# A fused attention and MLP block on one core: the first 220 jobs of a written-out job order in another sequence

## The chip, the core and the metric

The kernel runs on one core of one Trainium2 chip. The core has five engines with instruction queues of their own, each worked off in order: PE (matmul; its weight loads are listed as PEld), DVE (vector), ACT (activations), POOL (GpSimd) and SP, which here only issues DMAs. The metric is the device time of one execution in microseconds, the median of several runs. The profile is of one further execution, recorded instruction by instruction.

## What is computed

With x of 2048 rows by 512 columns, normalised to xn, the output is x + A(xn) + B(xn):

```python
# A: 32 heads of 16, 4 segments of 512 rows
q, k, v = heads(xn @ wq), heads(xn @ wk), heads(xn @ wv)
for s in range(4):
    p = softmax(q[s] @ k[s].T * scale + causal_mask)
    a_mem = (phi(q[s]) @ M) / (phi(q[s]) @ z + 1e-6)
    o[s] = g * a_mem + (1 - g) * (p @ v[s])
    M += phi(k[s]).T @ v[s];  z += phi(k[s]).sum(rows)
A = concat(o) @ wo
# B: a layer norm of its own, then two dense layers of width 1792
B = gelu(layernorm(xn) @ w1 + b1) @ w2 + b2
```

## The kernel before

**Split operands.** Products run as three float16 matmuls. Every weight and every row of xn is scaled and split into a high half and a low half in float16, and `split3` (L474 to L481) multiplies high by high, high by low and low by high into one PSUM bank. A group of 12 matmuls is thus a product over 512 inputs.

**What a weight needs first.** A weight matrix is loaded (`wl`, L245), its sum of squares is taken on ACT (`wm`, L311, each with a read-out of the accumulator), PE adds the sums over partitions by a matmul with ones and ACT takes a root (`wf`, L317 to L357: PE L326, L343 and L345, ACT L320 and L321, then short DVE operations), and then each piece of 128 rows or columns is split (`ws`, L359). There are two ways of splitting, by a letter in `SPLIT`: "V" is ACT L366 for the high half and DVE L367 for the low one; "G" is POOL L369 (scale), ACT L370 (high), POOL L371 (low). The weights come as the parts qk (first group of wq and wk), QK (the other three groups), v, 1a and 1b (the halves of w1), 2a and 2b (of w2), and o.

**The work.** Rows go in 4 segments of 512, heads in 4 groups of 8, so that there are 16 units (segment, group). For a unit, `T` projects k or q (`qk_proj`, L506: PE L480, ACT L514 and for a mapped k or q L517, DVE L518 to L530, and three stores to a scratch buffer in DRAM, from which four loads bring both back in another layout). `N` transposes phi(k), `V` projects v for 128 rows (PE L480 with wvs, ACT L593), `K` updates the state (PE L602). `M` finds row maxima of the scores (PE L621, DVE L628, 12 jobs a unit), `R` turns them (PE L499 with mc) and sends them through DRAM, `S` takes the exponentials (PE L661, ACT L666, POOL L675), `pv` and `PV` multiply by v (PE L690), and `O` normalises. For the MLP, `D` is one group of 12 matmuls of the first layer (PE L480 with w1s, DVE L756), `G` the gelu on ACT, `H` its split (POOL L770 and L772, ACT L771), and `e` a step of the second layer (PE L797). `X` and `Xt` normalise and transpose the rows, `ratio` lays out the row scales of the second norm, `gate` computes the gates from beta, and `warm` is eight matmuls of ones with no use of the result (L823).

**What sets the order.** No scheduler does. The kernel has 28 streams of jobs, each with a letter (`streams`, L57). `ORDER` is a string of 1307 letters: at each letter the next job of that stream is recorded on whichever engines it needs, and every engine keeps that order. `BANKS` is a string of digits that says, at each taking of a PSUM bank, which of the eight it is. The jobs are numbered from 0 here. Up to job 219 the kernel loads, checks and splits nearly all weights, projects units 0 and 1, finds their maxima and starts the exponentials and the MLP. Among the letters are a (norm), c (loads of weights), f and g (key and query projection), t (warm-up) and u to B (squares, scale and splits, one letter for each part of the weights).

```python
    for c in "".join(ORDER):
        key = next(todo[NAMES.index(c)])
```

Of the kernel before, what the change touches and what calls it, by code (L numbers as in the profile page):

```python
# [56 lines left out]
def streams():  # L57
# [42 lines left out]


ORDER = (
    "aatcucuccvavtctveecttcetcuvaactvuvtaatcattavdtubcwwvccfwxxcxwxyxyxxgyhxcoxxvwxofooowcvwzyzoiyyiazgyyziiynzoiiys"
    "ppAnziiniicvzvcniiooAzmAihiiopzqqiqcivpqjpqjijqqijizqjiqqjiiAwszBzoAskkkkmjiAojoijsoAijAqjqjasAfoAopgkkkkpjpjqq"
    "jlpoolojjjooilihAAkkkkpaiqqiqijqjqqijqjiqjqjisBfgpiiqkkkkmpliqqiooiqpBlqoBopohijjiojiijpolsjiqaqajqiqiqqiiqapka"
    "kmkktspaqijqiqjqiqajqbqajopijjgBfopkkkBkjjjlooooBlhjjjolqiqqiipkkkkjiqqijqqjjiqiqjjqiqiqiBkkkkmpliilfnplimpngrr"
    "mrjjponijqjqjinjipiskmkkmkaiijrijjoojiqsjqqjiqiiiqqkkkkihlqlfmlogojqjqjqqjjasoojmkkkkmqjiqjqjjaojjpipmooisikkkk"
# [9 lines left out]


BANKS = (
    "012345670123457063571265407321640573216405732164053271640527163054271630542713605427105472105427105472105472015"  # L120
    "470251407251405712470512470512470536124075631254076340125637123756123576132576132576132576132576135402761350427"
    "163054273106542736574326574326537425632754632574631072456310724563071245360712453620731620731067203617621073621"
    "073621073621037621037621037261702361475023671540263701524603175246031746013746013713460713471630471630463714067"
    "314056723410523674105236741052367410527410527410527410527410527140352671450326475103264751023674523674523647253"
# [786 lines left out]
```

## Time and profile before

| | us |
|---|---|
| median of 3 runs | 694.91 (694.29 to 697.16) |
| span of the profiled execution | 693.1 |
| PE busy | 678.7 (98%) |
| DVE busy | 535.4 (77%) |
| ACT busy | 522.7 (75%) |
| POOL busy | 347.2 (50%) |
| mean granted clock of PE | 0.995 |

The page states no time of the profiled execution beside its span; the span, from the first to the last instruction, is 1.8 us below the median of the runs. A row of the time line has the start, the time taken, the engine, the line of the kernel, the operation, output and inputs, the number of instructions merged in it, and in brackets the idle time of the engine ahead of it with what ended it. Times are from the start of the span.

### The profile page before, as it was taken

The numbers are of one execution on the slowest core, as the hardware profiler recorded it, in microseconds if no ns is written. First come the engines' busy times: TensorE is split into PE (matmuls) and PEld (weight loads), VectorE is DVE, ScalarE is ACT, GpSimd is POOL, SyncE is SP. The second block draws the span as 40 slices with busy tenths as digits, with TensorE's granted clock in tenths as the row PEclk, the third lists the DMA queues.
The fourth block names the chain that finished last, engine by engine and source line by source line (L and its number), as shares of the span: only waits on it lengthen the run. The fifth ranks groups of instructions, "written<-read, shape, count | busy, mean of one in ns | idle before, by whom it ended". The sixth has DMA issues, their size and how long they took to land.

```text
span 693.1 us, 16949 instructions
## 1 busy us (share of the span) xinstructions
PE 678.7 (98%) x6359; PEld 395.7 (57%) x6359; DVE 535.4 (77%) x1695; ACT 522.7 (75%) x1013; POOL 347.2 (50%) x533
## 2 busy tenths in 40 slices
PE   7799999999999999999999999999999999999997
PEld 6465556576654555566554456567564456656653
DVE  4499978897795887998798786888678595969442
ACT  5989898878795659857795697757795687778870
POOL 5276768365624425664334445454362546455752
PEclk9899999999999999999999999999999999999999
DMA  9984222420204213431113224231120416140101
GB/s 272 283 238 136 64 63 63 108 62 14 84 10 115 87 44 74 100 71 33 51 45 92 63 72 99 63 93 33 31 80 24 132 18 152 18 108 3 18 1 61
DMA packets 51790, 55.12 MB, mean 80 GB/s; under 512 B 4782, under 2 KB 40636, under 8 KB 51708
## 3 DMA queue, kind: packets, MB, share of 16 engines
q1 hardware_dynamic: 49404, 49.84, 25.3%
q0 software_dynamic: 2304, 4.20, 3.7%
q8 instruction: 50, 0.82, 0.5%
q14 instruction: 32, 0.26, 0.1%
HBM read 36.99 MB, written 17.04 MB: 78 GB/s over the span
## 4 chain that ended last, share of the span: by engine, by line
PE 78%; ACT 10%; POOL 4%; DVE 3%; issue 2%; DMA 1%; SPq 1%; POOLq 0%; ACTq 0%; DVEq 0%
PE ps L480 33%; PE ps L797 16%; PE ps L690 10%; PE ps L815 6%; PE ps L661 5%; PE ps L621 5%; ACT pt L666 2%; DVE ps L628 2%; PE ps L571 2%; PE ps L499 1%; ACT hT L763 1%; ACT hT L771 1%; SPq L252 1%; POOL w1s L371 1%; DMA pt<-in_A_wk_dram 1%
## 5 line engine op out<-in xcount | busy, mean ns | idle before, releaser
L628 DVE CUSTOM_DVE_ANT_0 ps<-ps,mask 128x512 f32<-128x512 f32 (+3 forms) x512 | 233.8, 522 | 16.1 <-PE ps L621 14.9
L666 ACT ACTIVATE pt<-ps,qkcs 128x512 f32<-128x512 f32 (+1 forms) x384 | 206.1, 624 | 35.3 <-PE ps L661 33.5
L797 PE MATMUL ps<-w2s,hT 64*128 64x512 f16 x1344 | 176.7, 376 | 0.2
L480 PE MATMUL ps<-xnT,w1s 128*128 128x256 f16 x1344 | 157.8, 273 | 0.0
L675 POOL TENSOR_SCALAR_AFFINE_SELECT pt<-pt 128x256 f32<-128x256 f32 x256 | 99.1, 414 | 92.0 <-ACT pt L666 91.0
L480 PEld LDWEIGHTS <-w1s 128*128 128x128 f16 x1344 | 127.3, 98 | 29.1 <-issue 11.3
L772 POOL TENSOR_TENSOR hT<-hh,hT 128x512 f16<-128x512 f32 x64 | 67.8, 1059 | 82.8 <-ACT hT L771 81.0
L797 PEld LDWEIGHTS <-hT 64*128 64x128 f16 x1344 | 76.3, 94 | 50.7 <-issue 6.0
L690 PE MATMUL ps<-pt,vt 128*32 128x512 f32 (+3 forms) x1024 | 77.3, 435 | 0.1
L756 DVE SCALAR_TENSOR_TENSOR hT<-ps,sc,sr 128x256 f32<-128x256 f32 x112 | 52.1, 478 | 27.2 <-PE ps L480 27.0
L628 DVE DVE_READ_ACCUMULATOR2_ANT mc<- 128x1 f32 x512 | 70.6, 138 | 0.0
L661 PE MATMUL ps<-qst,kst 50*128 50x512 f16 (+3 forms) x512 | 67.5, 298 | 0.3 <-ACT pt L666 0.2
L621 PE MATMUL ps<-kst,qst 48*128 48x256 f16 (+3 forms) x512 | 67.1, 297 | 0.5
L771 ACT ACTIVATE hT<-hh 128x512 f16<-128x512 f32 x64 | 36.6, 572 | 33.4 <-POOL hh L770 32.9
L690 PEld LDWEIGHTS ps<-pt,vt 128*32 128x32 f32 x1024 | 31.3, 109 | 42.4 <-issue 30.8
L770 POOL TENSOR_SCALAR hh<-hT,sc 128x512 f32<-128x512 f32 x64 | 41.8, 653 | 26.6 <-ACT hT L763 24.9
L720 POOL TENSOR_TENSOR nN<-nN,oT 128x512 f32<-128x512 f32 x16 | 20.3, 1267 | 61.3 <-DVE oT L546 61.3
L763 ACT ACTIVATE hT<-hT,b1t 128x256 f32<-128x256 f32 x112 | 46.4, 495 | 0.2
L480 PE MATMUL ps<-xnT,wqs 128*128 128x512 f16 x192 | 45.6, 389 | 0.0
L480 PE MATMUL ps<-xnT,wks 128*128 128x512 f16 x192 | 44.3, 379 | 0.0
L480 PE MATMUL ps<-wvs,xnT 128*128 128x512 f16 x192 | 44.0, 380 | 0.1
L815 PE MATMUL ps<-wos,oT 128*128 128x512 f16 x192 | 43.2, 380 | 0.6 <-POOL oT L726 0.6
(217 smaller groups left out, 890.0 us busy)
## 6 DMA issues: line engine op xcount, KB each, us to landing
kd<-hl SPq DMA_DIRECT2D x48, 128.0 KB
qd<-hl SPq DMA_DIRECT2D x48, 128.0 KB
kst<-kd SPq DMA_DIRECT2D x32, 192.0 KB
qst<-qd SPq DMA_DIRECT2D x32, 192.0 KB
acc<-in_A_x_dram SPq DMA_DIRECT2D x16, 256.0 KB
acc<-in_B_b_dram POOLq DMA_DIRECT2D x16, 256.0 KB, 4.1
out_dram<-acc SPq DMA_DIRECT2D x16, 256.0 KB
xt<-in_A_x_dram SPq DMA_DIRECT2D x14, 256.0 KB
```

Of the source, the lines that this page charges most:

```text
L480: T.matmul(p, wsl(ws, k, a), xsl(xs, k, b), start=s0 and i == 0, stop=s1 and i == 3 * n - 1)
L621: T.matmul(p[:, o:o + n], stk[i, 0][r, t, P * qb:P * qb + P], stk[i, 1][r, t, :n], start=True, stop=True)
L628: V.tensor_tensor_reduce(p[:, o:o + n], p[:, o:o + n], mask[:, 512 - n:], 1.0, -3e38, OP.add, OP.max, mc[:, 16 * b + 4 * t + qb:16 * b + 4 ...
L661: T.matmul(p[:, o:o + n], stk[i, 1][r, t, P * kb:P * kb + P], stk[i, 0][r, t, P * kb:], start=True, stop=True)
L666: A.activation(e[:, OFF[kbs[0]]:OFF[kbs[0]] + o], p[:, :o], AF.Exp, scale=qkcs[:, 1, i % NG:i % NG + 1])
L675: G.affine_select(v, v, pattern=[[0, 2], [1, P]], compare_op=OP.is_ge, fill=0.0, base=0, channel_multiplier=-1)
L690: T.matmul(p[32 * c:32 * c + 32, P * kb:], vt[s, kb][:, 4 * g + c, 16 * odd:16 * odd + 32], pt[i, 2 * c + odd][:, OFF[kb]:OFF[kb] + LEN[kb ...
L756: V.scalar_tensor_tensor(hz[:, fi, :], p[:, :256], col(F1 + fh), srow[hs][:, own], op0=OP.mult, op1=OP.mult)
L763: A.activation(z, z, AF.Gelu_apprx_tanh, bias=b1t[:, FH * (j % 2) + f:FH * (j % 2) + f + 1])
L772: G.tensor_tensor(hT[:, z, 1, :], t, hT[:, z, 0, :], op=OP.subtract)
L797: w = T.matmul(pes[j][a], hTs[fh][r, fi, u, P * a:P * a + P], w2s[r, fo, v, :], start=n == 0 and m == 0, stop=fi == FH - 1 and m == 2, ski ...
L815: T.matmul(p, o[:, u, P * b:P * b + P], wos[:, g, v, :], start=i == 0, stop=i == 3 * NG - 1)
```

## The change

Two rows of each table change; the 220 jobs are the same, in another sequence, and the digits of the banks follow it. From job 220 on both tables are as they were, and so is all code.

```diff
 ORDER = (
-    "aatcucuccvavtctveecttcetcuvaactvuvtaatcattavdtubcwwvccfwxxcxwxyxyxxgyhxcoxxvwxofooowcvwzyzoiyyiazgyyziiynzoiiys"
...
+    "aeactcacccuuaacttvtctuvvtaaavvvuecetcvuwtvatwccvwvwwcvdwfwgxtxtcxxycwxxyxxhnboyxfxyooynoxiiicoyytczivzigcizooyv"
...
```

In words, the jobs that move furthest. Ahead of the first projection now stand the norm of the first rows (statistics from job 10 to 6, application from 27 to 12), the split of wq's second group (75 to 47), those of the third group of wk and wq (85 to 49 and 122 to 53) and three of the four splits of wv; the fourth (86 before) stands between the two projections. The second projection (job 67 before) is job 58, right behind the first (54, now 56). The squares of w1 (56 before) come behind it, at 59. The first value projection moves from 104 to 75, the row ratios from 47 to 76, the gates from 172 to 68, the second half's w1 load from 53 to 63, and one warm-up block from 45 to 96. The loads of the second segment's first rows move from 95 to 170, those of wo from 125 to 167 and from 146 to 213.

On PE, around the first two projections: before, the first projection (wks) is followed by the scales of wv (first L343) and of w1 (second L343 and L345), and then the second projection (wqs), the scale of w2 and the transposes of phi(k).

```order
L433 MATMUL ps7_378<-ident_74,rat_111 128x128 x4
L480 MATMUL ps1_393<-xnT_287,wks_100 128x512
L343 MATMUL ps2_416<-am_105,ones_79 128x1 x2
L343 MATMUL ps6_431<-am_105,ones_79 128x1 x2
L345 MATMUL ps6_431<-am_105,ones_79 128x1
L480 MATMUL ps5_453<-xnT_287,wqs_99 128x512
L343 MATMUL ps4_476<-am_105,ones_79 128x1 x2
L499 MATMUL ps0_486<-ident_74,phk_408 128x64
L480 MATMUL ps3_504<-xnT_287,w1s_103 128x256
```

Now, on PE at the same place (each L480 row stands for 12 matmuls, each L828 row for 8):

```order
L343 MATMUL ps1_348<-am_105,ones_79 128x1 x2
L480 MATMUL ps3_378<-xnT_244,wks_100 128x512
L480 MATMUL ps6_403<-xnT_244,wqs_99 128x512
L828 MATMUL ps5_427<-ones_79 128x256
L343 MATMUL ps7_449<-am_105,ones_79 128x1 x2
L345 MATMUL ps7_449<-am_105,ones_79 128x1
L499 MATMUL ps3_484<-ident_74,phk_393 128x64
L480 MATMUL ps6_496<-wvs_101,xnT_244 128x512
L433 MATMUL ps0_511<-ident_74,rat_111 128x128 x4
L480 MATMUL ps2_517<-xnT_244,w1s_103 128x256
L343 MATMUL ps4_531<-am_105,ones_79 128x1 x2
```

The scale of wv moved ahead of both projections, which are neighbours now; two warm-up blocks (one of them shown), the scale of w1, a value projection and the ratios stand ahead of the first MLP group, and the scale of w2 behind it.

On ACT, the rows behind the squares of wv. Before, the first projection's evictions (hl, phk) come at once, and the squares of w1 ahead of the first split of wv:

```order
L370 ACTIVATE wks_100<-wks_100 128x512
L514 ACTIVATE hl_406<-ps1_393 128x512
L517 ACTIVATE phk_408<-ps1_393,qksc_107 128x512
L320 ACTIVATE fa_419<-ps2_416,sc_106 128x1
L311 ACTIVATE w1s_103,am_105<-w1s_103 128x1792 x2
L366 ACTIVATE wvs_101<-wvs_101,sc_106 128x512
L311 ACTIVATE w2s_104,am_105<-w2s_104 128x1792
```

Now, on ACT from the second square of wv to the first of w2:

```order
L311 ACTIVATE wvs_101,am_105<-pt_210 128x1024
L366 ACTIVATE wqs_99<-wqs_99,qksc_107 128x512
L370 ACTIVATE wks_100<-pt_169 128x512
L366 ACTIVATE wvs_101<-wvs_101,sc_106 128x512
L366 ACTIVATE wqs_99<-pt_171,qksc_107 128x512
L366 ACTIVATE wvs_101<-pt_210,sc_106 128x512
L514 ACTIVATE hl_391<-ps3_378 128x512
L517 ACTIVATE phk_393<-ps3_378,qksc_107 128x512
L514 ACTIVATE hl_416<-ps6_403 128x512
L311 ACTIVATE w1s_103,am_105<-w1s_103 128x1792 x2
L311 ACTIVATE w2s_104,am_105<-w2s_104 128x1792
```

Seven splits of wq, wk and wv and the second projection's eviction now stand ahead of the squares of w1 (rows that repeat are left out).

On PE between the first row-maximum jobs (L621), now: behind the fifth MLP group stands a warm-up block of eight matmuls, which before stood ahead of the first projection.

```order
L621 MATMUL ps3_649<-kst0_91,qst0_89 128x256
L480 MATMUL ps1_658<-xnT_244,w1s_103 128x256
L828 MATMUL ps6_677<-ones_79 128x256
L621 MATMUL ps7_688<-kst0_91,qst0_89 128x512
L621 MATMUL ps6_689<-kst0_91,qst0_89 128x512
```

All matmuls and all bytes moved are the same as before.

More of the change, by code (lines that the diff above doesn't have):

```diff
@@ L102 @@
 ORDER = (
-    "aatcucuccvavtctveecttcetcuvaactvuvtaatcattavdtubcwwvccfwxxcxwxyxyxxgyhxcoxxvwxofooowcvwzyzoiyyiazgyyziiynzoiiys"
-    "ppAnziiniicvzvcniiooAzmAihiiopzqqiqcivpqjpqjijqqijizqjiqqjiiAwszBzoAskkkkmjiAojoijsoAijAqjqjasAfoAopgkkkkpjpjqq"
+    "aeactcacccuuaacttvtctuvvtaaavvvuecetcvuwtvatwccvwvwwcvdwfwgxtxtcxxycwxxyxxhnboyxfxyooynoxiiicoyytczivzigcizooyv"
+    "zyyizppniniiiqqzizApmoihiAzioqiizAqpjoAsiozqijiqjmjipjsocAjaqBiizAkskkkiAqjqqzijojqijAqjajfAAssgoopkpkckkjopjqq"
     "jlpoolojjjooilihAAkkkkpaiqqiqijqjqqijqjiqjqjisBfgpiiqkkkkmpliqqiooiqpBlqoBopohijjiojiijpolsjiqaqajqiqiqqiiqapka"
@@ L119 @@
 BANKS = (
-    "012345670123457063571265407321640573216405732164053271640527163054271630542713605427105472105427105472105472015"
-    "470251407251405712470512470512470536124075631254076340125637123756123576132576132576132576132576135402761350427"
+    "662010636134154103657737602454361702543167602543170642304165762310457620457602465702476502476502467502467520467"
+    "502467502456704256704256705426470536124075631254076340125637123756123576132576132576132576132576135402761350427"
     "163054273106542736574326574326537425632754632574631072456310724563071245360712453620731620731067203617621073621"
```

## The prediction

> **What bounds the kernel now.** I read the page first, then busy time by stretches, then the time line of PE and ACT up to 110 us, since all that moves lies there.
>
> ```profile
> span 693.1 us, 16949 instructions
> PE 678.7 (98%) x6359; PEld 395.7 (57%) x6359; DVE 535.4 (77%) x1695; ACT 522.7 (75%) x1013; POOL 347.2 (50%) x533
> ...
> 20.00:25.00 5.00, 2.59 (x14) 1.44 (x12) 2.89 (x15) 4.94 (x10) 1.80 (x2) 0.97 1.10 345
> 25.00:30.00 5.00, 2.82 (x10) 1.91 (x11) 2.04 (x9) 4.75 (x10) 0.12 (x1) 0.50 1.11 343
> 30.00:35.00 5.00, 4.69 (x32) 2.82 (x31) 1.07 (x3) 4.97 (x10) 2.98 (x4) 0.84 0.46 137
> 55.00:60.00 5.00, 5.00 (x30) 1.94 (x28) 5.00 (x23) 5.00 (x11) 2.39 (x3) 1.00 1.01 274
> 120.00:693.00 573.00, 568.14 (x5398) 325.98 (x5394) 444.26 (x1393) 418.62 (x804) 273.93 (x427) 1.00 0.24 62
> ```
>
> Behind a stretch and its length stand PE, PEld, DVE, ACT, POOL, then the granted clock, the DMA share and GB/s. The kernel has two regimes. Up to about 33 us PE waits (2.59 and 2.82 of 5 busy, the second at half clock) while ACT is full. Behind that PE is full, to the end (568.14 of 573 after 120). A job order for the first 105 us therefore pays in one way only: PE enters its full stretch with more, or less, of its work behind it. The lag that PE has at job 220 is carried to the end, as the jobs behind are the same and PE has no idle time to give back. In before PE comes to that job here:
>
> ```profile
> 102.93 1.46 PE L797 MATMUL ps<-w2s,hT 64*128 64x512 f16 x12
> ```
>
> What PE waits for early:
>
> ```profile
> 19.18 2.91 PE L480 MATMUL ps<-xnT,wks 128*128 128x512 f16 x12
> 25.95 0.59 PE L343 MATMUL ps<-am,ones 128*128 128x1 f32 x2 [3.31 <-ACT w1s L311]
> 27.77 0.59 PE L343 MATMUL ps<-am,ones 128*128 128x1 f32 x2 [1.23 <-ACT w1s L311]
> 28.64 1.87 PE L480 MATMUL ps<-xnT,wqs 128*128 128x512 f16 x4
> 33.56 0.47 PE L499 MATMUL ps<-ident,phk 64*128 64x64 f32 x8
> 33.96 2.79 PE L480 MATMUL ps<-xnT,w1s 128*128 128x256 f16 x24
> 48.18 2.76 PE L480 MATMUL ps<-wvs,xnT 128*128 128x512 f16 x12
> ```
>
> The second projection (wqs, 28.64) stands behind the scale of the MLP weights (L343 at 27.77), which waits for ACT's squares of w1s; it runs at half clock and is through only at 32.7. From 33.56 nothing stops PE: an MLP group of 12 takes half of 2.79 less the drain, 1.3 us, and a value projection 2.6 (2.76 with its drain).
>
> **The change, by ACT's queue.** ACT works in order and is full early, so I add up its queue as it stands now. Its rows overlap by 0.1 (22.62 + 0.58 is 23.20, the next starts at 23.10); I count start to start.
>
> ```profile
> 8.07 0.53 DVE L396 TENSOR_SCALAR nw<-ag 128x4 f32<-128x4 f32 x1
> 9.81 0.63 ACT L311 ACTIVATE wks<-wks 128x512 bf16<-128x512 f32 x1 [0.27 <-DMA wks<-in_A_wk_dram]
> 13.16 0.80 ACT L411 ACTIVATE nN<-nN,stats 128x512 f32<-128x512 f32 x1
> 16.41 2.01 ACT L469 ACTIVATE xnT<-ps 128x512 f16<-128x512 f32 x4
> 19.88 1.05 ACT L311 ACTIVATE wvs<-wvs 128x1024 bf16<-128x1024 f32 x1
> 21.05 1.06 ACT L311 ACTIVATE wvs<-pt 128x1024 bf16<-128x1024 f32 x1
> 22.10 0.61 ACT L370 ACTIVATE wks<-wks 128x512 f16<-128x512 f32 x1
> 22.62 0.58 ACT L514 ACTIVATE hl<-ps 128x512 f16<-128x512 f32 x1
> 23.10 0.68 ACT L517 ACTIVATE phk<-ps,qksc 128x512 f32<-128x512 f32 x1
> 23.67 0.26 ACT L320 ACTIVATE fa<-ps,sc 128x1 f32<-128x1 f32 x1
> 24.10 1.70 ACT L311 ACTIVATE w1s<-w1s 128x1792 bf16<-128x1792 f32 x1
> 25.92 1.70 ACT L311 ACTIVATE w1s<-w1s 128x1792 bf16<-128x1792 f32 x1
> 29.22 1.68 ACT L311 ACTIVATE w2s<-w2s 128x1792 bf16<-128x1792 f32 x1
> 37.79 0.71 ACT L366 ACTIVATE wqs<-wqs,qksc 128x512 f16<-128x512 f32 x1
> ...
> 37.02 1.16 POOL L371 TENSOR_TENSOR w1s<-w1s 128x512 f16<-128x512 f32 x1 [0.74 <-ACT w1s L370]
> ```
>
> *To the first projection.* The norm's two activations now head the queue and wait for DVE's 8.07 + 0.53 = 8.6. Then come that pair (0.4, as the root pair from 23.67 to 24.10), eight squares of 0.63, read-out included (5.0), two norm rows L411 (1.4), two root pairs (0.8), two splits L366 (1.2), four xnT evictions (1.9), two value squares of 1.17 (2.3) and one L370 (0.5): 13.5 us, so 22.1. PE's first projection now stands behind the value weights' scale (0.59, plus 0.2 for a small transpose). It starts at 22.9 instead of 19.18 and ends at 25.6; the second follows at once and ends at 28.2 instead of 32.7.
>
> *To the MLP scale.* From 22.1 ACT has six L366 and one L370 (two pieces of wq, one of wk, all four of the value weights: 4.2), a root pair (0.4) and the first projection's evictions (0.5 + 0.6), to 27.8; it waits 0.4 for the second projection and evicts it, to 28.7. Two w1s squares of 1.82, the bias square (0.2) and its read-out (0.2) end at 32.75; in before the root of that scale could be taken after 28.05. The last of the scale's matmuls follow, about 0.7: 33.45. The two warm-up blocks behind the second projection (0.9 each) end near 29.9, so PE idles 2.9 us there.
>
> *To the full stretch.* PE has phk's transposes (0.45, to 33.9), the first value projection (36.5), the row of ratios (four transposes, 0.5, to 37.0) and the first MLP group. Its weights: root pair to 33.85, a w2s square of 1.68 (35.5), 0.1, L370 to 36.1, then POOL's low half of 1.16: 37.3. The group starts on its high half and ends at 38.5. The w2s scale needs the second w2s square (an L366 of 0.6 and 1.7 behind that L370, with its read-out 38.55), and PE is through it at 39.0. In before PE would have the same work done at 33.56 + 0.4 + 1.3 + 2.6 = 37.9, the ratios having fitted into an earlier gap. **Lag: +1.1.**
>
> *A warm-up block in the full stretch.* One of the 14 blocks now stands between an MLP group and the scores, where PE is full:
>
> ```profile
> 9.84 1.91 PE L828 MATMUL ps<-ones 128*128 128x256 f16 x16
> ```
>
> Half of it, less the drain, is about **+0.9** for its eight; bounds 0 (if PE waits for a bank there anyway) and 0.95.
>
> *Behind the first scores.* The row maxima's transposes (L499, mc) need DVE's last read of the 12 score jobs.
>
> ```profile
> 63.55 2.79 PE L480 MATMUL ps<-xnT,w1s 128*128 128x256 f16 x24
> 66.13 0.87 DVE L756 SCALAR_TENSOR_TENSOR hT<-ps,sc,sr 128x256 f32<-128x256 f32 x2
> 66.27 0.55 PE L602 MATMUL ps<-vt,pkn 128*32 128x48 f32 x32
> ```
>
> DVE is through 2.6 us after PE wrote the last scores (63.55 to 66.13). Two MLP groups and the state update, 3.2 us, covered that; now one group and the update do, 1.85. So up to +0.75 is exposed; but two second-layer steps (1.3 us) now stand just ahead of the last score job and let DVE catch up. I take **+0.2**, nearer the covered end.
>
> *At nothing.* The gates (six short DVE operations) move to about 34 us, into DVE's idle time (1.07 busy of 30 to 35). SP's loads of the second half of w1 now stand behind the second projection's three stores and four loads, issued by about 33; their squares come on ACT near 50, and the DMA share was only 0.46 in 30 to 35. If that cover failed, ACT would wait, not PE at once. The loads of later x rows and of wo move back, but are used long behind. Bounds: 0 to 0.5.
>
> The sum is 1.1 + 0.9 + 0.2 = +2.2 on the profiled span of 693.1, that is 695.3; the runs' median, 694.91, lies 1.8 above that span, and gets the same 2.2: **697.1**. The first term is a difference of two sums of some thirty starts; I give it 1.5 either way.
>
> **Rivals.** *The clock falls in the new gap (slower).* The clock by single microseconds:
>
> ```profile
> 22.00:23.00 1.00, 0.59 (x5) 0.41 (x3) 0.00 (x0) 1.00 (x4) 0.20 (x1) 1.00 1.07 359
> 24.00:25.00 1.00, 0.00 (x0) 0.00 (x0) 0.97 (x3) 1.00 (x2) 0.00 (x0) 0.87 1.05 389
> 31.00:32.00 1.00, 1.00 (x4) 0.35 (x3) 0.00 (x0) 1.00 (x2) 0.40 (x1) 0.72 0.79 227
> ```
>
> PE stopped at 22.59; the clock was coming down before 25 and came back only in the slice from 31, although PE was full from 28.64. The new gap, 29.9 to 32.8 and then only small matmuls to 33.9, is as long. If the clock falls there, the first value projection runs half slow until the clock is back, some 3 us as above: half of its 2.6 lost, +1.3, so 698.4; it decides if the clock is down by 34. If the gap ahead of the first projection does the same to both, ACT waits for their evictions and 2.6 more is lost: 701.
>
> [...]
>
> *ACT falls behind in the full stretch (slower).* ACT now holds the second value eviction ahead of three splits by POOL's way, and PE reaches that projection only at 44 to 47, so ACT idles up to 1.7 there; and two such splits now stand next to each other, so ACT waits for POOL's 1.16 and 0.7 between them, 1.9 more. ACT was 5.00 busy of 5 in 55 to 60, so 3.6 lost may come out at the exponentials: 697.1 + 3.6 = 700.7 at worst.
>
> *DVE and ACT, not PE, pace the stretch from 45 to 65 (faster).* All three read 5.00 of 5 in 55 to 60. Work that now lies ahead (a value split 0.6, one of wq and one of wk 1.1, a value eviction 0.5, about 2.3 us on ACT) would then shorten it and hide the lag: 694.9 - 2.3 = 692.6. Against it: PE shows no idle time there, so its busy time would have to be partly stretched.
>
> **Chances.** The sum as forecast 0.45; the clock 0.27; ACT behind 0.10; the faster pacing 0.18. A measurement of this kernel tells about 0.5% from no change, that is 3.5 us: 691.4 to 698.4. The forecast lies within, save 0.03; the clock case falls beyond in 0.22 of its 0.27, ACT in 0.08 of 0.10; the faster case in 0.10 of 0.18, where the first term errs the same way. Faster 0.10, same 0.57, slower 0.33. For 8 in 10 I take 692.0 to 701.0, from just below the faster case to the end of the clock case.
>
> **What would show it.** The first projection near 22.9, the second right behind it at full clock; the w1s scale's matmuls near 33 with a wait of about 3 us on ACT L311; the w2s scale near 39; a warm-up block near 50 with no idle time ahead of it; the pair of second-layer steps (102.93 in before) near 105. I am wrong if PE comes to that pair before 103: then either the ACT sum is too long or PE was not the bound.

## Result and profile after

| | before | after |
|---|---|---|
| median of 7 runs each, us | 695.04 (694.29 to 697.16) | 699.54 (698.05 to 700.41) |
| ratio, with its 95% interval | 1 | 1.0058 (1.0048 to 1.0068) |
| span of the profiled execution, us | 693.1 | 697.8 (that run took 699.54) |
| PE busy, us | 678.7 | 682.9 |
| start of the first row-maximum job on PE (first L621) | 44.51 | 50.08 |
| start of the row maxima's transposes (L499, mc) | 66.75 | 71.34 |
| start of the pair of second-layer steps at job 220 | 102.93 | 107.82 |

The changed kernel is 4.5 us slower: inside the range and to the side forecast, at twice the +2.2 of the sum, and just beyond the 0.5% that the forecast called no change. The page of after, and two stretches of it with the columns of the prediction's first fence:

```profile
span 697.8 us, 16953 instructions
PE 682.9 (98%) x6359; PEld 396.0 (57%) x6359; DVE 534.6 (77%) x1695; ACT 523.0 (75%) x1013; POOL 348.9 (50%) x533
...
30.00:35.00 5.00, 3.50 (x18) 2.28 (x19) 1.67 (x7) 4.26 (x10) 0.70 (x1) 0.69 0.61 183
35.00:40.00 5.00, 5.00 (x22) 2.52 (x21) 3.88 (x8) 5.00 (x11) 3.40 (x4) 0.63 0.98 225
```

PE is busy 4.2 us longer with the same 6359 instructions. The last two stretches show why: the granted clock was 0.69 and 0.63 there (before: 0.84 and 1.00), and the twelve matmuls of the first value projection count as busy for 5.25 us, where they take 2.76 in before (48.18, at a clock of 1.00). The clock had also fallen once ahead of that, to 0.50 from 15 to 20 us, but was back when the first projection began (1.00 from 22 us on). Rows of PE's time line of after:

```profile
22.24 2.76 PE L480 MATMUL ps<-xnT,wks 128*128 128x512 f16 x12
24.84 2.75 PE L480 MATMUL ps<-xnT,wqs 128*128 128x512 f16 x12
29.96 0.38 PE L343 MATMUL ps<-am,ones 128*128 128x1 f32 x2 [0.62 <-ACT w1s L311]
31.78 0.48 PE L343 MATMUL ps<-am,ones 128*128 128x1 f32 x2 [1.44 <-ACT w1s L311]
33.68 5.25 PE L480 MATMUL ps<-wvs,xnT 128*128 128x512 f16 x12
40.51 0.50 PE L343 MATMUL ps<-am,ones 128*128 128x1 f32 x4
50.08 0.72 PE L621 MATMUL ps<-kst,qst 48*128 48x512 f16 x8
52.05 1.04 PE L828 MATMUL ps<-ones 128*128 128x256 f16 x8
67.71 0.40 PE L621 MATMUL ps<-kst,qst 48*128 48x384 f16 x4 [0.74 <-DVE mc L628]
71.34 0.27 PE L499 MATMUL ps<-ident,mc 64*96 64x64 f32 x2
107.82 1.46 PE L797 MATMUL ps<-w2s,hT 64*128 64x512 f16 x12
```

Both projections run back to back at a clock of 1.00 (22 to 30 us), and the scale of w1 waits for ACT's squares as forecast, though for 2.1 us (0.62 and 1.44) and not 2.9. Then comes the slow value projection (33.68). The lag at the job-220 pair is 107.82 - 102.93 = 4.9 us, and it stays to the end (span +4.7, median +4.5).

**Where the 4.9 us arise**, from starts in the two time lines. PE comes to its first row-maximum job 5.57 us later. Of these, 2.6 are work: two value projections (5.2 us) now stand ahead of it, and two MLP groups fewer (2.6). The other 3.0 are lag, where 1.1 was forecast. From there to the row maxima's transposes PE takes 21.26 us (before 22.24); less the 2.6 of work it would have been 19.64, so 1.6 are lost. Two rows above add up to that: the warm-up block at 52.05 (an estimate of 0.9, as sixteen matmuls took 1.91 in before and eight take 1.04 here) and the wait of 0.74 us at 67.71. From the transposes to the pair 36.48 us go by instead of 36.18: 0.3. So 3.0 + 1.6 + 0.3 = 4.9.

### The profile page after: what moved, and what is told of

Its sections match the earlier page's. It is cut to its first block, busy times and chain, and to the rows that moved or that the text cites. A ratio compares the mean times of both kernels' runs of the same rounds, so it can differ in the third digit from the quotient of the medians.

```text
span 697.8 us, 16953 instructions
## 1 busy us (share of the span) xinstructions
PE 682.9 (98%) x6359; PEld 396.0 (57%) x6359; DVE 534.6 (77%) x1695; ACT 523.0 (75%) x1013; POOL 348.9 (50%) x533
## 4 chain that ended last, share of the span: by engine, by line
PE 83%; ACT 7%; DVE 5%; issue 2%; DMA 1%; POOL 1%; POOLq 0%; SPq 0%; DVEq 0%; ACTq 0%
PE ps L480 36%; PE ps L797 16%; PE ps L690 10%; PE ps L815 6%; PE ps L621 5%; PE ps L661 5%; DVE ps L628 3%; PE ps L571 2%; ACT pt L666 1%; PE ps L499 1%; DVE mc L628 1%; DMA nN<-in_A_x_dram 1%; ACT hT L771 1%; PE ps L602 1%; DMA qst<-md 0%
## 5 line engine op out<-in xcount | busy, mean ns | idle before, releaser
L628 DVE CUSTOM_DVE_ANT_0 ps<-ps,mask 128x512 f32<-128x512 f32 (+3 forms) x512 | 234.1, 523 | 17.4 <-PE ps L621 16.1
L480 PE MATMUL ps<-xnT,w1s 128*128 128x256 f16 x1344 | 158.5, 273 | 0.0
L480 PEld LDWEIGHTS <-w1s 128*128 128x128 f16 x1344 | 127.2, 98 | 29.8 <-issue 12.0
L628 DVE DVE_READ_ACCUMULATOR2_ANT mc<- 128x1 f32 x512 | 71.2, 139 | 0.0
L621 PE MATMUL ps<-kst,qst 48*128 48x256 f16 (+3 forms) x512 | 66.6, 297 | 1.5 <-DVE mc L628 0.7
L480 PE MATMUL ps<-wvs,xnT 128*128 128x512 f16 x192 | 46.5, 395 | 0.0
L480 PE MATMUL ps<-xnT,wqs 128*128 128x512 f16 x192 | 44.2, 380 | 0.0
L480 PE MATMUL ps<-xnT,wks 128*128 128x512 f16 x192 | 44.1, 379 | 0.0
L621 PEld LDWEIGHTS <-qst 48*128 48x128 f16 x512 | 28.0, 94 | 28.4 <-issue 14.7
```

What stands on the lines that cost most here:

```text
L480: T.matmul(p, wsl(ws, k, a), xsl(xs, k, b), start=s0 and i == 0, stop=s1 and i == 3 * n - 1)
L621: T.matmul(p[:, o:o + n], stk[i, 0][r, t, P * qb:P * qb + P], stk[i, 1][r, t, :n], start=True, stop=True)
L628: V.tensor_tensor_reduce(p[:, o:o + n], p[:, o:o + n], mask[:, 512 - n:], 1.0, -3e38, OP.add, OP.max, mc[:, 16 * b + 4 * t + qb:16 * b + 4 ...
```

## Experiments

My theory was: PE is the bound, the clock took some 2 us ahead of the first scores, the warm-up block 0.9 behind them. The rivals: what PE wins early is taken back by another engine; or each part of the move costs by itself. Each experiment was timed against the kernel before on its own chip (medians there 695.02 to 695.64). Where jobs move, the digits of their banks move along. Starts of rows in the profiled runs, for all of them:

| kernel | first L621 | mc transposes | job-220 pair | median us | ratio (95%) |
|---|---|---|---|---|---|
| before | 44.51 | 66.75 | 102.93 | 695.04 | 1 |
| after | 50.08 | 71.34 | 107.82 | 699.54 | 1.0058 (1.0048 to 1.0068) |
| w10_fill | 48.26 | 69.52 | 107.67 | 699.87 | 1.0065 (1.0053 to 1.0077) |
| clk_held | 48.30 | 69.56 | 106.03 | 698.68 | 1.0055 (1.0043 to 1.0067) |
| w11_out | 51.31 | 72.53 | 109.02 | 699.79 | 1.0062 (1.0049 to 1.0074) |
| clk_held_w11 | 48.23 | 69.44 | 105.93 | 699.12 | 1.0066 (1.0053 to 1.0079) |
| dve_less | 48.42 | 69.89 | 106.61 | 699.30 | 1.0057 (1.0045 to 1.0069) |
| t00_only | 48.40 | 72.25 | 108.26 | 700.00 | 1.0066 (1.0054 to 1.0079) |
| vsplit_only | 49.18 | 71.01 | 107.10 | 699.57 | 1.0062 (1.0050 to 1.0075) |
| t00_behind_sq | 46.57 | 70.41 | 106.43 | 698.77 | 1.0049 (1.0036 to 1.0061) |
| before_clk | 46.54 | 70.40 | 106.60 | 696.24 | 1.0028 (1.0014 to 1.0043) |
| t00_t11_gap | 43.57 | 70.61 | 106.63 | 697.29 | 1.0038 (1.0024 to 1.0052) |
| v_in_gap | 49.74 | 70.95 | 108.77 | 700.61 | 1.0083 (1.0070 to 1.0096) |
| v01_back | 45.22 | 76.21 | 112.72 | 706.65 | 1.0163 (1.0146 to 1.0179) |

### The clock

One gap filled, the block behind the second projection made longer:

```diff
-        for _ in range(8):
+        for _ in range({10: 32}.get(n, 8)):
```

> The changed kernel with 32 instead of 8 matmuls in the second warm-up block behind the second projection, so that PE stays busy from 28.3 to 31.8 us, where it idled and the clock fell. Clock theory (the fall costs time): no half clock behind the second projection, the first value projection in 2.8 us instead of 5.1, and 1.4 to 2.6 us less than the changed kernel's 699.5: 697.0 to 698.1. Rival (ACT's queue sets the start of PE's full stretch and hides the slow projection): 699.5, no change.

PE's time line of w10_fill:

```profile
34.20 2.76 PE L480 MATMUL ps<-wvs,xnT 128*128 128x512 f16 x12
...
69.52 0.26 PE L499 MATMUL ps<-ident,mc 64*96 64x64 f32 x2
...
75.56 0.39 PE L661 MATMUL ps<-qst,kst 50*128 50x512 f16 x1 [1.01 <-DMA qst<-md]
76.19 0.39 PE L661 MATMUL ps<-qst,kst 50*128 50x512 f16 x1 [0.24 <-DMA qst<-md]
```

The value projection is back at 2.76 us and the transposes come 1.8 us earlier than in after. Then PE waits 1.25 us for the row maxima to come back from DRAM, and the pair is where it was in after. SP's queue shows that trip, first in after, then in w10_fill: the store to md is issued, and the loads behind it wait for it to land (1.1 us in after, 2.9 in w10_fill).

```profile
72.64 0.33 SPq L641 DMA_DIRECT2D md<-mhl  x1
74.07 0.55 SPq L644 DMA_DIRECT2D qst<-md  x2
```

```profile
70.80 0.33 SPq L641 DMA_DIRECT2D md<-mhl  x1
74.03 0.55 SPq L644 DMA_DIRECT2D qst<-md  x2
```

From the store to the loads it took 1.4 us in after, and 3.2 in w10_fill. The DMA views of 68 to 78 us show one difference: in w10_fill a 16 KB packet of an instruction queue (0.6% of the 16 engines' time in these 10 us, so about 1 us on one of them) falls into the same slices as the store, 71.5 to 73.0, where 33 KB were moved; in after the store's 16 KB stand alone, from 73.4 to 73.7. So this loss goes with another transfer that fell on the store, and not with PE's earlier start as such: in clk_held, below, the transposes come as early (69.56), and the pair at 106.03. All early gaps were filled next, to see the clock alone:

```diff
-        for _ in range(8):
+        for _ in range({6: 32, 8: 20, 10: 32}.get(n, 8)):
```

> The changed kernel with three of its early warm-up blocks made longer (32, 20 and 32 matmuls instead of 8), so that PE has work in every gap ahead of the full stretch; all else as changed. Theory 1 (the clock is most of the loss): the half-clock stretch at the value projection goes for every run, and nothing takes it back: 697.0 to 698.1 us, 1.4 to 2.6 less than the changed kernel. Theory 2 (what PE wins early is lost again at the waits between the first scores and the row maxima, as in the run that filled one gap): 699.5 us, and the wait of the second score block for the row maxima's loads is longer than 0.5 us.

In the profile of clk_held the clock is 1.00 in every stretch from 5 to 110 us and all three marks of the table are 1.8 us earlier than in after; no wait takes it back. The timed runs show less: 1.0055 against 1.0058, no difference that the intervals can tell, and a median above the range of theory 1. A likely reason is seen in the single runs of after. Four had a mean clock of 0.990 and took 699.5 to 700.4 us; three had 0.994 or 0.995 and took 698.05 to 698.7. With the clock held the five took 698.2 to 699.4. So within after the lower clock goes with some 1.4 us more, in about half of its executions. By an estimate from these figures (0.0045 of 697.8 us, at half clock) the faster runs have some 6.3 us less of half clock, about one fall; which of the two falls of the profiled run it is, no run shows. The other 3 to 3.5 us are there with the clock held too.

### The warm-up block in the full stretch

Cut to one matmul, in after and in clk_held:

```diff
-        for _ in range(8):
+        for _ in range({11: 1}.get(n, 8)):
```

> The changed kernel with one matmul instead of eight in the warm-up block that stands between an MLP group and the scores (52.05 to 53.02 us). If PE's work is the bound there, 0.75 to 0.95 us less: 698.7. Rival (DVE's reading of the scores paces PE there, and the block stands in a wait): 699.5, no change.

> As the kernel with the three longer blocks, and the warm-up block in the full stretch cut from 8 matmuls to 1. If PE's work alone bounds the stretch: 0.9 us less than that kernel, near 696.2 to 697.2. If the waits behind the first scores take up what PE wins: no difference between the two, and the wait ahead of the row maxima's transposes is about 0.9 us longer here.

w11_out's marks come late because its clock was at half from about 16 to 26 us (0.50 in 20 to 25, 0.85 in 25 to 30) and the first projection took 4.52 us instead of 2.76; its stretch from the first L621 to the transposes, 21.22 us, and its median, 699.79, show no gain. The second run is the clean one. PE of clk_held_w11:

```profile
51.46 0.38 PE L621 MATMUL ps<-kst,qst 48*128 48x384 f16 x3 [0.51 <-DVE mc L628]
...
65.81 0.40 PE L621 MATMUL ps<-kst,qst 48*128 48x384 f16 x4 [0.74 <-DVE mc L628]
...
69.44 0.26 PE L499 MATMUL ps<-ident,mc 64*96 64x64 f32 x2
```

From the first L621 to the transposes PE takes 21.21 us without the block's 0.9 us, and 21.26 with it. In its place PE waits 0.51 us for DVE to read the scores and free the bank, and the wait of 0.74 further on stays; where the remaining 0.3 go, the rows do not show. Taking the block out won nothing.

Next, is it DVE? DVE reads the scores from its first L628 to its last in 20.5 us in after and in all five timed kernels of its order. In clk_held_w11 the reads of the first score block were made shorter (the kernel leaves out the maxima over the columns beyond 256):

```diff
+                    c = min(n, 256) if i == 0 else n
                     for b, p in enumerate(ps):
-                        V.tensor_tensor_reduce(p[:, o:o + n], p[:, o:o + n], mask[:, 512 - n:], 1.0, -3e38,
+                        V.tensor_tensor_reduce(p[:, o:o + c], p[:, o:o + c], mask[:, 512 - c:], 1.0, -3e38,
```

> The run with the three longer blocks and the short one in the full stretch, and besides DVE's row-maxima reads of the first score block cut to at most 256 columns (the maxima over the columns beyond are left out), which takes about 3 us of DVE's work out between the first scores and the row maxima's transposes; PE's work is the same. DVE theory (from the first score block DVE sets the pace: 20.5 us from its first read to its last in every kernel of the changed order so far): the transposes come 1.2 to 1.6 us earlier, at about 68 instead of 69.44 us, to the point where PE's own work (about 19.7 us there) bounds, and the time falls by as much, to 696.7 to 697.9. PE theory (PE's work bounds there): no change.

The row of PE that speaks against both, in dve_less:

```profile
68.69 1.26 PE L480 MATMUL ps<-xnT,w1s 128*128 128x256 f16 x10 [0.62 <-POOL w1s L371]
```

The wait of 0.51 us is gone and PE is some 0.6 us further on at 65, counted from the first L621. Then an MLP group waits 0.62 us for POOL's low half of w1, and the transposes come 21.47 us behind the first L621: nothing is won, nor in the median. POOL is itself 0.35 us later with that half than in clk_held_w11, counted from the first L621, as two of its scalings (L369, at 52.13 and 57.91) overlap splits of DVE and took 1.25 and 1.13 us instead of 0.70. My DVE theory fell too, as a single bound: with less work on PE, DVE holds PE; with less on DVE, the splits do.

Nor does DVE work through the whole stretch. DVE of after:

```profile
63.87 0.57 DVE L628 CUSTOM_DVE_ANT_0 ps<-ps,mask 128x384 f32<-128x384 f32 x1 [0.40 <-PE ps L621]
...
66.78 0.43 DVE L628 CUSTOM_DVE_ANT_0 ps<-ps,mask 128x256 f32<-128x256 f32 x1 [1.27 <-PE ps L621]
```

Twice DVE stands for scores, each time while PE does a value projection, and right behind the second PE stands 0.74 us for DVE (67.71). Waits like these are in clk_held, clk_held_w11 and dve_less (there 1.53 us on DVE and 0.75 on PE, although the reads are shorter). In before neither engine waits in this stretch. So PE and DVE hold each other up in the new order. Which part of the order does it is not shown: in before, too, two value projections (57.15 and 60.43) have only four score matmuls between them, and there neither engine waits.

Last, in clk_held_w11, the second value projection was moved back behind four row-maximum jobs:

```diff
-    "aeactcacccuuaacttvtctuvvtaaavvvuecetcvuwtvatwccvwvwwcvdwfwgxtxtcxxycwxxyxxhnboyxfxyooynoxiiicoyytczivzigcizooyv"
+    "aeactcacccuuaacttvtctuvvtaaavvvuecetcvuwtvatwccvwvwwcvdwfwgxtxtcxxycwxxyxxhnboyxfxyooyoxiiicoyytczinvzigcizooyv"
```

> The run with the three longer blocks and the short one in the full stretch, and the second value projection (2.6 us of PE) moved back behind the first four score steps. DVE theory: the first scores come 2.6 us earlier, PE's work from there to the transposes grows from 19.6 to 22.2 us and now exceeds DVE's 20.5, so the transposes come 1.0 to 1.6 us earlier (near 68 instead of 69.44) and the time falls by as much, to 697.5 to 698.1. PE theory (all that counts is PE's total work up to there): no change.

It took 706.65 us, ratio 1.0163 (1.0146 to 1.0179), and tells nothing of either theory (PE):

```profile
53.85 4.44 PE L480 MATMUL ps<-wvs,xnT 128*128 128x512 f16 x12 [3.91 <-DVE mc L628]
```

The projection took its bank, 6, along to a place right behind the row-maximum job that writes banks 7 and 6. It had to wait for DVE to read them, 3.91 us, and it then took 4.44 us instead of 2.76. My estimate is that this was the clock, as that run's mean was 0.997 and clk_held's 1.000; where in the run it was low is not shown. So it stays open how much of the 1.6 us behind the first scores the places of the projections cost.

### Each part alone

The second projection alone, in the kernel before, right behind the first:

```diff
-    "aatcucuccvavtctveecttcetcuvaactvuvtaatcattavdtubcwwvccfwxxcxwxyxyxxgyhxcoxxvwxofooowcvwzyzoiyyiazgyyziiynzoiiys"
+    "aatcucuccvavtctveecttcetcuvaactvuvtaatcattavdtubcwwvccfgwxxcxwxyxyxxyhxcoxxvwxofooowcvwzyzoiyyiazgyyziiynzoiiys"
```

> The kernel before with one part of the change alone: the second projection right behind the first, nothing else moved. Theory (PE waits for ACT's squares of w1 and w2 up to 33.25 us in any case, and the second projection lies in that wait wherever it stands): no change, 694.5 to 695.5; if the longer wait lets the clock fall later, up to 696.5. Rival (its 4.0 us at half clock are on the path): 691 to 693.7.

It cost 4.4 us, more than either expectation allowed. ACT, then PE, of t00_only:

```profile
24.92 0.60 ACT L514 ACTIVATE hl<-ps 128x512 f16<-128x512 f32 x1 [0.94 <-PE ps L480]
25.41 0.26 ACT L320 ACTIVATE fa<-ps,sc 128x1 f32<-128x1 f32 x1
25.70 0.20 ACT L321 ACTIVATE fa<-fa 128x1 f32<-128x1 f32 x1
25.84 1.70 ACT L311 ACTIVATE w1s<-w1s 128x1792 bf16<-128x1792 f32 x1
```

```profile
36.13 4.51 PE L480 MATMUL ps<-xnT,w1s 128*128 128x256 f16 x24
...
61.87 0.38 PE L621 MATMUL ps<-kst,qst 48*128 48x384 f16 x3 [0.90 <-DVE mc L628]
...
72.25 0.26 PE L499 MATMUL ps<-ident,mc 64*96 64x64 f32 x2 [0.41 <-DVE mc L628]
```

Three prices show. ACT waits 0.94 us for the projection's end and evicts it, so that the squares of w1 start at 25.84 instead of 24.10. PE's gap is now emptier, the granted clock is 0.50 from 30 to 35 us and 0.53 from 35 to 40, and the first 24 matmuls of the MLP take 4.51 us instead of 2.79: the first L621 is 3.9 us late. And behind it PE waits twice for DVE, 1.3 us.

The value splits alone, ahead of the squares of w1:

```diff
-    "aatcucuccvavtctveecttcetcuvaactvuvtaatcattavdtubcwwvccfwxxcxwxyxyxxgyhxcoxxvwxofooowcvwzyzoiyyiazgyyziiynzoiiys"
+    "aatcucuccvavtctveecttcetcuvaactvuvtaatcattavdtubcwwvccfwwwwwxxcxxyxyxxgyhxcoxxvxofooocvzyzoiyyiazgyyziiynzoiiys"
```

> The kernel before with the other part alone: the four splits of the value weights ahead of the squares of w1, nothing else moved. Theory (ACT's queue up to the w2 squares sets the start of PE's full stretch): four splits of 0.6 ahead of the squares put the scales of w1 and w2 2.4 us later, and PE's full stretch with them: 697.0 to 697.6. Rival (only ACT's total counts, as the splits vanish from 38 to 43 us): 695.0, no change.

It cost 3.9 us, more than the 2.4 that the theory had. ACT of vsplit_only:

```profile
25.56 1.33 ACT L366 ACTIVATE wvs<-wvs,sc 128x512 f16<-128x512 f32 x2 [1.75 <-DVE sc L349]
27.10 1.38 ACT L366 ACTIVATE wvs<-pt,sc 128x512 f16<-128x512 f32 x2 [0.21 <-DVE wvs L367]
28.39 1.68 ACT L311 ACTIVATE w1s<-w1s 128x1792 bf16<-128x1792 f32 x1
```

ACT stands 1.75 us for the scale of wv, which DVE takes only behind its part of the first projection's eviction. With that and the four splits the squares start 4.3 us late (28.39 instead of 24.10), and the transposes of phi(k) 4.7 us late (38.23 instead of 33.56). The second projection ahead of them ran at half clock here as well (0.50 from 30 to 35 us; 5.05 us, 4.18 in before).

So each part alone costs about what the whole change costs. They are not two terms of a sum: in each of the three kernels ACT's squares of w1 start late (28.13 in after, 25.84 and 28.39 alone, 24.10 in before), PE takes up its work at a lower clock in after and t00_only (0.63 and 0.53 from 35 to 40 us), and the first L621 comes late (5.6, 3.9 and 4.7 us).

To take ACT's wait away, the second projection was put behind the squares and ahead of their scale:

```diff
-    "aatcucuccvavtctveecttcetcuvaactvuvtaatcattavdtubcwwvccfwxxcxwxyxyxxgyhxcoxxvwxofooowcvwzyzoiyyiazgyyziiynzoiiys"
+    "aatcucuccvavtctveecttcetcuvaactvuvtaatcattavdtubcwwvccfwxxcxgwxyxyxxyhxcoxxvwxofooowcvwzyzoiyyiazgyyziiynzoiiys"
```

> The kernel before with only the second projection moved, but not right behind the first: it stands behind ACT's squares of the MLP weights and ahead of their scale, so that PE can do it in its gap while ACT goes on with the squares. Theory 1 (moving the projection cost 4.4 us because ACT's queue waited for it, 0.94 us, and had to evict it before the squares): ACT starts the squares at 24.1 as before; but for the clock, which falls in the gap that the projection leaves at 28.6, the time is that of before: 695 to 696.5. Theory 2 (the clock in that gap is the cost): half of the first MLP groups' 4 to 5 us is slow, 697.5 to 699.5.

It took 698.77, inside the range of theory 2, but by what follows only about half of the loss is the clock's. PE of t00_behind_sq:

```profile
34.45 4.35 PE L480 MATMUL ps<-xnT,w1s 128*128 128x256 f16 x24
...
60.03 0.38 PE L621 MATMUL ps<-kst,qst 48*128 48x384 f16 x3 [0.90 <-DVE mc L628]
...
70.41 0.27 PE L499 MATMUL ps<-ident,mc 64*96 64x64 f32 x2 [0.41 <-DVE mc L628]
```

ACT is undisturbed (its squares start at 23.96), and still the first 24 MLP matmuls take 1.6 us more (4.35 instead of 2.79). By my estimate this is the clock, whose mean was 0.992 here and 0.995 in before. The first L621 is 2.1 us late. At the transposes it is 3.7. The other 1.6 us come from DVE, whose reads take 21.8 us here, as in t00_only and before_clk, and 19.9 in before. Of the same jobs three rows are longer. DVE and POOL of t00_behind_sq, first of the three:

```profile
49.69 1.44 DVE L367 SCALAR_TENSOR_TENSOR w2s<-w2s,sc 128x512 f16<-128x512 f32 x1
```

```profile
49.43 1.15 POOL L371 TENSOR_TENSOR w2s<-w2s 128x512 f16<-128x512 f32 x1 [0.74 <-ACT w2s L370]
```

and the same split of DVE in before, with POOL's nearest row:

```profile
47.52 0.74 DVE L367 SCALAR_TENSOR_TENSOR w2s<-w2s,sc 128x512 f16<-128x512 f32 x1
```

```profile
48.38 1.16 POOL L371 TENSOR_TENSOR w2s<-w2s 128x512 f16<-128x512 f32 x1 [0.74 <-ACT w2s L370]
```

In before DVE's split takes 0.74 us, and no add of POOL overlaps it. Issued while POOL adds, it takes 1.44 and ends at 51.13; less 0.74 that is 50.39, within 0.2 us of POOL's end (50.58). The other two longer rows (53.15 and 66.40) come as close to the ends of POOL's adds (53.65 and 67.50), as if DVE had stood until POOL was almost through; by which means is not shown. Three such meetings (1.44, 1.05 and 1.64 us instead of 0.74) make the 1.9 us. In these kernels a shift of 2.1 us ahead of the scores (first L621) thus became 3.7 us at the transposes.

### The clock in before, and two tries at a better kernel

In before, one warm-up block moved into the gap behind the first projection and made longer:

```diff
-    "aatcucuccvavtctveecttcetcuvaactvuvtaatcattavdtubcwwvccfwxxcxwxyxyxxgyhxcoxxvwxofooowcvwzyzoiyyiazgyyziiynzoiiys"
+    "aatcucuccvavtctveecttcetcuvaactvuvtaatcattavdubcwwvccfwtxxcxwxyxyxxgyhxcoxxvwxofooowcvwzyzoiyyiazgyyziiynzoiiys"
...
-        for _ in range(8):
+        for _ in range({11: 32}.get(n, 8)):
```

> The kernel before with one of its warm-up blocks moved into the gap behind the first projection and made longer (32 matmuls instead of 8), so that the clock is kept for the second projection, which then ends near 31.2 instead of 32.7 us. Theory 1 (before, the slow clock lay under a wait for ACT's squares of w2, and cost nothing at the end): 694.7 to 695.6 us, no change to the kernel before, but for 0.9 us less because the block is out of the full stretch. Theory 2 (the slow clock cost there too): 693.0 to 694.2 us.

The second projection did end 1 us earlier, and PE then waited 1.77 us for ACT's squares of w2, and the clock fell there instead (0.93 from 30 to 35 us, 0.73 from 35 to 40). PE of before_clk:

```profile
33.65 0.38 PE L343 MATMUL ps<-am,ones 128*128 128x1 f32 x2 [1.77 <-ACT w2s L311]
...
34.35 4.42 PE L480 MATMUL ps<-xnT,w1s 128*128 128x256 f16 x24
```

Seven of the twelve runs took 694.5 to 696.4 us at a mean clock of 0.998, five 698.5 to 699.3 at 0.997. A difference of 0.001 of 697 us is 0.7 us (1.4 at most, with the rounding), so the clock does not account for the 3 us between the groups. The profiled run is of the upper group, with the three meetings of DVE and POOL in it (1.44, 1.05 and 1.65 us); the lower group has no profile, so that these are the cause is not shown. In before, the slow clock (0.50 from 25 to 31 us) lay under the second projection (4.18 us), which ACT's squares covered: this is the mechanism of theory 1, though the median is 0.6 us above its range, and there is no gain.

In clk_held, real work put into the gap in place of a longer block:

```diff
-    "aeactcacccuuaacttvtctuvvtaaavvvuecetcvuwtvatwccvwvwwcvdwfwgxtxtcxxycwxxyxxhnboyxfxyooynoxiiicoyytczivzigcizooyv"
+    "aeactcacccuuaacttvtctuvvtaaavvvuecetcvuwtvatwccvwvwwcvdwfwgxtxtcxnxycwxxyxxhbfoyxxyooynoxiiicoyytczivzigcizooyv"
...
-        for _ in range(8):
+        for _ in range({6: 32, 8: 20, 10: 1, 11: 1}.get(n, 8)):
```

> The changed kernel with the first value projection moved ahead of the MLP weights' scale, into the gap where PE waits for ACT's squares, the second half of the keys' steps one place earlier, the two longer blocks ahead of it kept and the other two cut to 1 matmul. If PE's work bounds from there to the end: 2.6 us of the value projection come out of the full stretch besides the clock's and the block's, 693.5 us, below the kernel before. If DVE and the row maxima's trip through DRAM pace the stretch: up to 696, and the waits at the second score block grow instead.

It took 700.61 us, missed by both theories. PE of v_in_gap:

```profile
41.81 4.10 PE L480 MATMUL ps<-xnT,w1s 128*128 128x256 f16 x24 [2.81 <-ACT fa L320]
...
76.89 0.79 PE L661 MATMUL ps<-qst,kst 50*128 50x512 f16 x2 [0.89 <-DMA qst<-md]
```

The 2.6 us won in the gap are lost at the next MLP groups: ACT takes the root of w2's scale at 41.49, behind the eviction of the projection that was moved up (41.14 in clk_held, so only 0.35 later), and PE, which has that projection behind it already, waits 2.81 us for the root, and the clock falls (0.66 from 40 to 45 us). The trip through DRAM costs 0.89 more, again with a 16 KB instruction packet in the slices of the store (73.0 to 74.25).

In before, both projections, the transposes of phi(k) and a warm-up block of 14 matmuls in the gap (the run "just above" in the expectation is t00_behind_sq):

```diff
-    "aatcucuccvavtctveecttcetcuvaactvuvtaatcattavdtubcwwvccfwxxcxwxyxyxxgyhxcoxxvwxofooowcvwzyzoiyyiazgyyziiynzoiiys"
+    "aatcucuccvavtctveecttcetcuvaactvuvtaatcattavdubcwwvccfwxxcxgwxyxyxxhftyxcoxxvwxoooowcvwzyzoiyyiazgyyziiynzoiiys"
...
-        for _ in range(8):
+        for _ in range({11: 14}.get(n, 8)):
```

> As the run just above, and besides the first group's transposes, the second projection of the keys (2.6 us of PE, ahead of the MLP groups instead of between them) and a warm-up block of 14 matmuls put into the gap that is left, so that the clock holds and PE's full stretch begins with 2.6 us less to do. If PE's work bounds: 692.5 to 694, below the kernel before. If ACT's splits of the MLP weights and DVE bound from 35 us on: 694.5 to 696, no better than before.

It took 697.29 us, above the range of the second theory but by its mechanism. PE of t00_t11_gap, in a run that took 698.77:

```profile
39.75 3.89 PE L480 MATMUL ps<-xnT,w1s 128*128 128x256 f16 x34 [1.64 <-DVE w1s L367]
...
53.74 0.38 PE L343 MATMUL ps<-am,ones 128*128 128x1 f32 x2 [1.12 <-ACT w1s L311]
...
70.61 0.26 PE L499 MATMUL ps<-ident,mc 64*96 64x64 f32 x2 [0.20 <-DVE mc L628]
```

PE waits 1.64 us for the splits of w1, which DVE does behind the projection's eviction, and still reaches its first L621 0.9 us before the kernel before does. It reaches its transposes 3.9 us behind it: in between it waits 1.12 us for the squares of w1's second half and 1.4 in four waits for DVE, and an MLP group takes 2.72 us instead of 1.47 (54.31). The last is by my estimate the clock, whose mean was 0.997 in that run; where it was low is not shown. No order tried here beats the kernel before.

## Why the prediction was right, and where it was off

- **To the first projection: 22.9 forecast, 22.24 measured.** The norm's pair on ACT came earlier than assumed. Right to 0.7 us, and so is what follows: the second projection ends near 27.6 (28.2), the scale of w1 is through at 32.7 (33.45), behind a wait on ACT's squares.
- **To the full stretch: +1.1.** PE was to be through the scale of w2 at 39.0; it is at 40.9. The value projection ahead of it took 2.5 us more by the clock, and the earlier start gave 0.7 back. With the clock held, the first L621 is 48.30 - 44.51 = 3.79 us behind before, where the sum gives 2.6 + 1.1 = 3.7, and the steps on the way agree: PE is through the scale of w1 at 33.50 (33.45 forecast) and of w2 at 39.23 (39.0). So this account of ACT's queue was right. That it agrees to 0.1 us is in part luck: the longer blocks of clk_held put its first projection at 22.83, near the forecast's 22.9, while after has it at 22.24.
- **The clock, a rival at 0.27 and +1.3.** It came in the profiled run and, by the mean clocks, probably in about half of the runs. The forecast rightly took this rival from the trace of before: in after PE's waits behind 29.3 were 0.62 and 1.44 us with small matmuls between, and the clock fell all the same. That the clock holds in this gap, as the sum took it, no run shows: in after it fell to 0.50 (32 to 38 us), and in w10_fill, with matmuls in the gap, it was 1.00 from 25 to 110 us. The fall ahead of the first projection came too, but ended at 21.7 us, before that projection, and did not cost the 2.6 us allowed for it. In the trace the loss was the whole 2.6 us of the value projection and not half of it, as the half clock lasted 6.8 us instead of some 3; over the runs the price of about 1.4 us was near the forecast's. That it belonged into the sum, and not beside it, is one of two steps that failed.
- **The warm-up block, +0.9: the step that was wrong.** The row stands as forecast (1.04 us, no idle ahead), and without it nothing is faster. The lower bound of 0 was the right end: taking the block out changed the stretch by 0.05 us. The premise behind it, that work on PE counts one to one because PE shows no idle time, does not hold from the first scores to the row maxima.
- **Behind the first scores, +0.2.** The wait came not at the transposes but ahead of a score job (67.71, 0.74 us on DVE). Block and wait together were to be 1.1 us; 1.6 were lost in that stretch. The experiments name no single engine that holds it: PE and DVE wait for each other there, and with less work on DVE the splits by ACT and POOL hold PE. With the clock held this stretch costs more than the one ahead of it (1.6 against 1.2), and its cause is left open in part.
- **At nothing.** The gates ran at about 35 us in DVE's idle time (1.67 of 5 busy in 30 to 35): right. From the transposes to the pair 0.3 us more, within the 0.5 allowed.
- **The other rivals.** ACT did not fall behind, but the faster pacing did not come either: ACT was 2.7 to 3.1 of 5 busy between 40 and 55 (4.4 to 4.7 before), so its work did shrink there, and PE gained nothing by it.

In sum: forecast +2.2; with the clock held about +3.5, and some 1.4 more with the lower clock in part of the runs, which makes the median +4.5. The range held because it reached to the end of the clock case. By the chances, what came (slower) had 0.33, behind 0.57 for no change.

## What to carry to other kernels

A full PE row is no proof that PE sets the pace: take work off it and see whether the next mark moves, since here 0.9 us less came out as 0.05. Where an order is written by hand, a projection that is moved up brings its eviction into the queue of the engine that was already full, so count first what stands behind it there (in t00_only the squares of w1 started 1.74 us later). A gap of PE that holds only single small matmuls should be priced with the clock in the sum: here the clock fell to 0.50 in such gaps of before, after and t00_only (though not in before_clk behind waits of 0.43 and 1.44 us), and in after the projection that followed took 5.25 us instead of 2.76.

## What the runs showed that was not expected

- The half-clock stretches had lengths near one, two, three and four times 3.4 us: worked out from the clock of the stretches up to 110 us, they were 3.4 us long in before_clk (0.93 and 0.73 from 30 to 40), 6.8 in before and twice in after, 10.3 in t00_only (0.94, 0.50 and 0.53 from 25 to 40) and 13.7 in vsplit_only (0.89, 0.50, 0.50 and 0.74 from 20 to 40). The mean clock differed between runs of one kernel (0.990 to 0.995 in after).
- Three of DVE's splits (L367) that overlap an add of POOL took 1.44, 1.05 and 1.64 us instead of 0.74 in t00_behind_sq, and the same reads of the scores took 21.8 us there and 19.9 in before.
- From a 16 KB store to DRAM to the issue of the load that waits for it, it took 1.4 us in before, after, w11_out, t00_only and vsplit_only, and 3.2 in w10_fill and 3.1 in v_in_gap. In these last two a 16 KB packet of an instruction queue falls into the slices of the store; in before and after none lies between the store and the load. No run moved that packet by itself, so that it is the cause is not shown.
